# Attention with a gated feed-forward block: the low part of the probabilities times the high part of v alone, in six matmuls a head, placed by the scheduler

## The chip, the cores and the metric

The kernel runs on one core of one Trainium2 chip. The metric is the device time of one execution in microseconds (us). The kernel before took 822.91 us, the median of three runs (821.95 to 823.51). The traces come from a separate profiled execution.

Engine names are those of the profile: PE is TensorE (matmuls), PEld its weight loads, DVE VectorE, ACT ScalarE, POOL GpSimd, SP SyncE, which here issues DMAs only.

## What is computed

The reference, cut to what matters, with 8 batches, 8 heads, 576 positions and a head dimension of 64:

```python
scores = scale * np.matmul(q, k.transpose(0, 1, 3, 2))
bias = -(cum[:, :, :, None] - cum[:, :, None, :])      # cum = cumsum(max(s, 0))
scores = np.where(causal, -1000000000.0, scores + np.minimum(bias, 0.0))
attn = np.exp(scores - max); attn = attn / (sum + 1e-09)
x = np.matmul(attn, v)                                 # heads side by side: (8, 576, 512)
h = gelu(x @ w_in)                                     # 512 -> 1024
u, v = halves of h
v_n = (v - mu) / np.sqrt(var + 1e-06) * g_ln
v_s = np.einsum('ts,bsd->btd', w_sg, v_n) + b_sg[None, :, None]
return x + (u * v_s) @ w_out
```

## The kernel before, in words

**The arithmetic.** The first 12 heads (`NP`, line 50) take their probabilities and v as plain float32. For the other 52 heads both are split: a float32 number is written as a high part, rounded to the type float32r, and a low part, the rest, also float32r. The product of two such numbers is then made of matmuls of parts. The feed-forward block works in such parts throughout, with three products of four (high·high, high·low, low·high).

**One head.** `scores` (line 713) makes the score matrix in strips in the PSUM buffers `sc`; DVE adds the mask and finds the extreme, ACT makes the exponentials into the SBUF tiles `p`. `transposes` (line 744) turns 12 blocks of 128x128 of `p` round on PE (`tr`, line 749: `p` is the weight operand of 128 columns, `ident` the moving operand of 128 columns), in four PSUM tiles `pt` of 4, 4, 2 and 2 blocks. The ring `pt` has two buffers. Each tile is evacuated by `evac` (line 759): ACT writes the high part (`pah`, `pbh`, `pdh`) and DVE the low part, PSUM minus high part (`pal`, `pbl`, `pdl`). Each of these SBUF tiles exists once, so the next head overwrites it. `pv` (line 807) multiplies by v. Its PSUM tile `xx` (128 rows, 512 columns) comes from a pool of one buffer (`ps_x`, line 446); the last 64 positions go to a tile `x0` (in the profile `x`) from the ring `pt`. The weights are `vs[:, jt]`, where 64 columns of high part and 64 columns of low part of v lie side by side. One matmul with 128 weight columns thus makes high-part sums in rows 0 to 63 and low-part sums in rows 64 to 127. The high part of the probabilities and then the low part stream against these 128 columns: of low parts four matmuls, of 512, 448, 320 and 192 columns. At the end ACT copies rows 64 to 127 to SBUF (tile `xr`) and DVE adds rows 0 to 63. After every second head POOL multiplies `xr` by the reciprocal sums.

**The feed-forward block** of a batch, `ffn` (line 861), consists of units v, u, s and o, each a chain of 12 to 14 matmuls into one of three PSUM buffers (`ps_m`), in the order of the string `ORDER` (line 42). The batch of eight heads before is in the feed-forward block while the next eight heads are in attention. Matmuls are of 128 weight columns and 288 or 512 moving columns. Only the last v unit, that of 64 positions, has in each batch four matmuls with 64 weight columns and 512 moving columns (line 910).

**The order of the work.** All operations are first recorded (`Program.add`) with a key, the time in heads at which they are due (`place`, line 1009, `POS`, line 58). `Program.graph` finds the dependencies; a PSUM buffer counts as one piece there, so any two accesses of which one writes stay in the order of the recording. `Program.cost` (line 189) gives each operation a duration `d` and for PE a load time. `plan` (line 308) is a greedy list scheduler: at each step it takes, over the five engines, the ready operation with the earliest start among up to 48 a queue, the earlier key first among equals. On PE an operation starts at

```python
s = max(pest + peocc, max(at[i], pest) + cost[i][2])
```

that is, when the matmul before it has streamed (`peocc` is its `d`) and its own weights, loaded from the start of that matmul on (`cost[i][2]`), are there. `emit` (line 275) issues everything in this order. The order on each engine is then fixed on the chip; only waits move. As all instructions are issued in `emit`, the profile gives line 289 for each of them, and one goes by the names of the tiles.

Two more features of `plan` are touched. Elementwise DVE operations that read and write SBUF alone are marked `wide`; `held` and `asked` put such an operation behind a POOL operation marked `lock` that runs at the planned time, and the other way round.

Of the kernel before, what the change touches and what calls it, by code (L numbers as in the profile page):

```python
# [21 lines left out]
P = 128  # L22
# [26 lines left out]
NQ = 8  # L49
NP = 12  # L50
U2 = 8
ENG = {'k': 'sg', 'vs': 'sg', 'xs': 'gg', 'ln': 'sg', 'gt': 'sg', 'w': 'gg', 'ws': 'sv', 'ws1': 'g'}
MT = 52.0
LATE = 0.0
# [12 lines left out]
OVERLAP = [0, 93, 75, 25, 0]  # L67
MARGIN = 100.0
ISSUE = 450.0


class Buf:
# [99 lines left out]
class Program:  # L172
# [16 lines left out]
    def cost(self, op):  # L189
        e, name, ins, outs, kw = op["eng"].n, op["name"], op["ins"], op["outs"], op["kw"]  # L190
        big = [v for v in ins if v.columns() > 1]
        n = outs[0].columns() if outs else big[0].columns()
        ps = [v.buf.pool.psum for v in big]
        ops_ = bool(outs) and outs[0].buf.pool.psum
        wide = lock = False
        d, load = 50.0, 0.0
        if e == PE:
            if name == "transpose":
                d, load = 110.0, 0.44 * ins[0].columns()
            else:  # L200
                w, m = ins
                load, n = 0.84 * w.columns(), m.columns()
                d = 0.463 * n if m.dtype == F32R else max(0.833 * n, load) + 0.833 * n
        elif e == ACT:
            f = kw.get("func")
            d = (195 if not any(ps) else 166) + 0.834 * n
            if f == AF.Exp:
                d = 480 + 0.834 * n
            elif f == AF.Tanh:
                d += 10  # L210
        elif e == DVE:
            d = 150 + 1.045 * n
            if name == "tensor_tensor_reduce":
                d += 7
            elif name == "reciprocal":
                d = 170
            elif name == "bn_stats":
                d = 687
            elif name == "bn_aggr":
                d = 172  # L220
            elif name == "memset":
                d = 60 + 0.8 * n
            elif n > 1 and not ops_ and not any(ps):
                wide = True
                if len(big) == 1:
                    d = 140 + 0.53 * n
        elif e == POOL:
            lock = n > 64
            if name == "tensor_tensor":
                d = (560 if kw["op"] == ALU.pow else 193) if n == 1 else 170 + 2.17 * n  # L230
            elif name == "tensor_scalar":
                d = 255 + 0.84 * n if n > 4 else 210
                if kw["op0"] == ALU.max:
                    d, lock = 3.3 * n, False
            else:
                d, lock = 140 + n, False
        else:
            v = (outs or big)[0]
            d, load = v.dims[0][1] * v.columns() * 4 / 280.0, ISSUE
        return e, d, load, wide, lock  # L240
# [65 lines left out]


def plan(cost, pre, first, uses, order, bufs, prio, after, slack=(0, 0, 0, 0, 0), window=48):

    n = len(cost)
    left = [len(p) for p in pre]
    succ = [[] for _ in range(n)]
    for i, p in enumerate(pre):
        for q in p:
            succ[q].append(i)
    issue = [[] for _ in range(n)]
    for i, qs in after.items():  # L320
        for q in qs:
            issue[q].append(i)
            left[i] += 1
    owner, remain = {}, {}
    for i in range(n):
        for b in first[i]:
            owner[b] = i
            left[i] += 1
        for b in uses[i]:
            remain[b] = remain.get(b, 0) + 1  # L330
    ready = [[] for _ in range(5)]
    at = [0.0] * n
    tagof = {b: t for t, bs in order.items() for b in bs}
    free_slots = {t: [0.0] * bufs[t] for t in order}
    nxt = {t: 0 for t in order}
    last = {}

    def put(j):
        left[j] -= 1
        if left[j] == 0:  # L340
            insort(ready[cost[j][0]], (prio[j], j))

    def grant(t):
        while free_slots[t] and nxt[t] < len(order[t]):
            b = order[t][nxt[t]]
            nxt[t] += 1
            f = free_slots[t]
            x = min(f)
            f.remove(x)
            j = owner[b]  # L350
            at[j] = max(at[j], x)
            put(j)

    for i in range(n):
        if left[i] == 0:
            insort(ready[cost[i][0]], (prio[i], i))
    for t in order:
        grant(t)
    free = [0.0] * 5
    start, fin = [0.0] * n, [0.0] * n  # L360
    pest = peocc = moved = 0.0
    held = asked = (0.0, 0.0)
    seqs = [[] for _ in range(5)]
    for _ in range(n):
        best = None
        for e in range(5):
            cand, least = [], 1e18
            for pr, i in ready[e][:window]:
                if e == PE:
                    s = max(pest + peocc, max(at[i], pest) + cost[i][2])  # L370
                    soon = pest + peocc + 1
                else:
                    s = max(at[i], free[e])
                    soon = free[e]
                cand.append((s, pr, i))
                least = min(least, s)
                if s <= soon:
                    break
            for c in cand:
                if c[0] <= least + slack[e]:  # L380
                    if best is None or c[0] < best[0]:
                        best = (c[0], e, c[1], c[2])
                    break
        if best is None:
            return None
        s, e, pr, i = best
        del ready[e][bisect_left(ready[e], (pr, i))]
        _, d, load, wide, lock = cost[i]
        if e == PE:
            pest, peocc, end = s, d, s + d + 60  # L390
            free[e] = s
        elif e == SP:

            moved = max(moved, s + 1300) + d
            free[e], end = s + load, moved + 600
        else:
            if e == DVE and wide and held[0] <= s < held[1]:
                s = held[1]
            if e == POOL and lock and asked[0] <= s < asked[1]:
                s = asked[1]  # L400
            end = s + d
            if wide:
                asked = (s, end)
            if lock:
                held = (s, end)
            free[e] = end - OVERLAP[e]
        start[i], fin[i] = s, end
        seqs[e].append(i)
        for j in issue[i]:
            at[j] = max(at[j], s)  # L410
            put(j)
        for j in succ[i]:
            ej = cost[j][0]
            at[j] = max(at[j], s if e == ej == PE else end + LATENCY[e][ej] + MARGIN)
            put(j)
        for b in uses[i]:
            remain[b] -= 1
            last[b] = max(last.get(b, 0.0), end)
            if remain[b] == 0:
                free_slots[tagof[b]].append(last[b] + 60)  # L420
                grant(tagof[b])
    return max(fin), start, fin, seqs
# [3 lines left out]
def tile_attn_gmlp(  # L426
# [380 lines left out]
    def pv(h):  # L807
# [5 lines left out]
        if key not in xr:  # L813
            xr[key] = moe.tile([P, S], F32, name="xr", tag="xr", bufs=8)
        xt = xr[key]
        parts = 1 if f32 else 2
        rows = D if f32 else P

        def st(jt):
            return d["v"][:, jt, :] if f32 else d["vs"][:, jt, :, :].rearrange("p a d -> p (a d)")  # L820

        xx = ps_x.tile([P, 512], F32, name="xx", tag="xx")

        def mm(o0, o1, jt, m, **kw):
            nc.tensor.matmul(xx[0:rows, o0:o1], st(jt), m, **{"start": False, "stop": False, **kw})

        m, pb, pd = pt["pa"], pt["pb"], pt["pd"]
        for k in range(parts):  # L830
            mm(0, 512, 0, m[k], start=(k == 0))
        yield 0.2
        for k in range(parts):
            mm(64, 512, 1, pb[k][:, 320:768])
        for k in range(parts):
            mm(128, 448, 2, pb[k][:, 0:320])
        yield 0.65
        mm(192, 384, 3, pd[0][:, 128:320])
        if not f32:
            mm(192, 384, 3, pd[1])  # L840
        x0 = ps_pt.tile([P, 512], F32, name="x0", tag="pt")
        if f32:
            nc.tensor.matmul(xx[0:rows, 256:320], st(4)[REM:P], pd[0][REM:P, 64:128], start=False, stop=True)
            nc.tensor.matmul(x0[0:rows, 0:64], st(5)[0:REM], pd[0][0:REM, 64:128], start=True, stop=True)
        else:
            mm(256, 320, 4, pd[0][:, 0:64], stop=True)
            nc.tensor.matmul(x0[:, 0:64], st(5), pd[0][:, 64:128], start=True, stop=True)
        hs = slice(64 * half, 64 * half + 64)
        for ps, o, sl in ((x0, slice(0, 64), slice(512, S)), (xx, slice(0, 512), slice(0, 512))):
            if f32:  # L850
# [257 lines left out]
```

## Time and profile before

| what | value |
|---|---|
| median of three runs | 822.91 us |
| the profiled execution | 821.75 us |
| its span, first to last instruction | 820.0 us |
| outside the span | 1.75 us |
| matmuls, and as many weight loads | 5129 |
| granted TensorE clock, mean | 0.997 |
| transposes, 128x128 | 768, mean 276 ns |
| low-part matmuls of 52 heads | 208 |

A matmul's duration in the profile runs from its issue to a modelled end, and matmuls overlap. What a matmul takes of the engine is read from the distance between starts in a timeline, not from its duration. A matmul that follows a transpose is recorded some 28 ns after the start of that transpose and then lasts longer. In rows such as `128*64 128x512` the first pair is weight rows and columns, the second the moving operand.

### The profile page before, as it was taken

How to read it: one execution, taken by the hardware profiler on the slowest of the kernel's cores; microseconds unless marked ns; L12 is line 12 of the kernel's file. 1: busy time of each engine (PE TensorE's matmuls, PEld its weight loads, DVE VectorE, ACT ScalarE, POOL GpSimd, SP SyncE). 2: the span in 40 equal slices, each digit the busy share in tenths (PEclk: the TensorE clock that was granted, in tenths of full speed). 3: DMA queues.
4: the chain of work that ended last, by engine and by line, in shares of the span. 5: the costliest groups of instructions: out<-in, count | busy, mean ns of one | idle time of the engine just before them, and what ended most of it. 6: DMA issues, size and time to landing. Idle time of an engine off the chain costs nothing.

```text
span 820.0 us, 16771 instructions
## 1 busy us (share of the span) xinstructions
PE 791.2 (96%) x5129; PEld 687.4 (84%) x5129; DVE 614.2 (75%) x1845; ACT 574.1 (70%) x1576; POOL 497.2 (61%) x767
## 2 busy tenths in 40 slices
PE   7999989999999999999999999999999999999998
PEld 4455557999988998899988998889988998889998
DVE  5798489877797678875788677976788767884662
ACT  4777679867787577876687677875778866872350
POOL 3676679584467555585476745675555854746442
PEclk9999999999999999999999999999999999999999
DMA  7576754555425654354535554256443546321101
GB/s 226 160 222 164 173 158 112 128 136 141 115 65 132 165 129 117 88 137 111 148 93 130 137 128 119 68 128 170 122 120 89 138 113 152 85 51 44 43 8 59
DMA packets 75566, 98.91 MB, mean 121 GB/s; under 512 B 27298, under 2 KB 43876, under 8 KB 75476
## 3 DMA queue, kind: packets, MB, share of 16 engines
q1 hardware_dynamic: 75476, 97.84, 45.7%
q8 instruction: 41, 0.67, 0.4%
q14 instruction: 49, 0.40, 0.2%
HBM read 51.71 MB, written 9.90 MB: 75 GB/s over the span
## 4 chain that ended last, share of the span: by engine, by line
PE 83%; DVE 7%; ACT 3%; DMA 3%; issue 3%; POOL 1%; SPq 0%; ACTq 0%; POOLq 0%; DVEq 0%
PE sm L289 13%; PE om L289 13%; PE sc L289 12%; PE vm L289 12%; PE xx L289 11%; PE um L289 10%; PE pt L289 10%; DVE p L289 2%; ACT p L289 1%; DMA raw<-in_kq 1%; PE x L289 1%; DVE u L289 1%; DVE bs L289 1%; DVE vm L289 1%; DVE vt L289 1%
## 5 line engine op out<-in xcount | busy, mean ns | idle before, releaser
L289 ACT ACTIVATE p<-p,mn 128x320 f32<-128x320 f32 (+4 forms) x320 | 177.8, 557 | 42.3 <-DVE mn L289 38.9
L289 PE MATMUL pt<-ident,p 128*128 128x128 f32 x768 | 156.6, 276 | 4.7 <-ACT pal L289 1.4
L289 DVE CUSTOM_DVE_ANT_0 p<-sc,mask 128x448 f32<-128x448 f32 (+4 forms) x320 | 125.2, 421 | 25.4 <-PE sc L289 22.9
L289 PE MATMUL sc<-k,q 66*128 66x288 f32 (+9 forms) x672 | 134.5, 307 | 2.2 <-DMA k<-cum 1.3
L289 PE MATMUL sm<-ws,vn 128*128 128x288 f32 x768 | 134.2, 304 | 2.3 <-DVE u L289 2.3
L289 PE MATMUL um<-xs,wi 128*128 128x288 f32 x768 | 132.0, 306 | 1.4 <-DVE u L289 1.1
L289 PE MATMUL om<-gt,wo 128*128 128x288 f32 x768 | 131.0, 307 | 0.0
L289 PE MATMUL vm<-wi,xs 128*128 128x512 f32 (+1 forms) x416 | 126.8, 408 | 0.1
L289 PEld LDWEIGHTS pt<-ident,p 128*128 128x128 f32 x768 | 97.6, 140 | 28.5 <-issue 5.6
L289 PEld LDWEIGHTS sm<-ws,vn 128*128 128x128 f32 x768 | 112.2, 188 | 6.3 <-DVE u L289 4.9
L289 PEld LDWEIGHTS um<-xs,wi 128*128 128x128 f32 x768 | 110.7, 189 | 4.2 <-DVE vt L289 2.1
L289 PEld LDWEIGHTS sc<-k,q 128*128 128x128 f32 (+3 forms) x672 | 101.4, 181 | 13.1 <-DVE mn L289 3.7
L289 PEld LDWEIGHTS om<-gt,wo 128*128 128x128 f32 x768 | 109.3, 189 | 1.1
L289 POOL TENSOR_TENSOR k<-raw,k 128x576 fp32r<-128x576 f32 x56 | 80.3, 1434 | 32.0 <-ACT k L289 19.7
L289 POOL TENSOR_TENSOR gt<-u,gt 128x288 fp32r<-128x288 f32 x64 | 50.8, 808 | 57.9 <-ACT gt L289 55.8
L289 PEld LDWEIGHTS vm<-wi,xs 128*128 128x128 f32 (+1 forms) x416 | 71.2, 185 | 10.8 <-DVE vt L289 0.4
L289 DVE SCALAR_TENSOR_TENSOR u<-u,um 128x288 f32<-128x288 f32 x128 | 56.5, 441 | 10.5 <-ACT u L289 10.2
L289 POOL TENSOR_SCALAR bs<-bs 128x1 f32<-128x1 f32 (+1 forms) x80 | 17.2, 215 | 77.3 <-DVE bs L289 74.1
L289 ACT CAST pbh<-pt 128x512 fp32r<-128x512 f32 x104 | 49.4, 481 | 19.5 <-PE pt L289 18.5
L289 POOL TENSOR_SCALAR p<-p 64x64 f32<-64x64 f32 x128 | 32.2, 252 | 49.4 <-ACT p L289 36.7
L289 POOL TENSOR_TENSOR xr<-xr,rb 128x576 f32<-128x576 f32 x32 | 46.1, 1441 | 24.0 <-DMA rb<-rd 20.6
L289 ACT ACTIVATION_READ_ACCUMULATOR p<-p,mn 128x1 f32 (+1 forms) x320 | 60.2, 188 | 0.0
(123 smaller groups left out, 1645.5 us busy)
## 6 DMA issues: line engine op xcount, KB each, us to landing
q<-k SPq DMA_DIRECT2D x168, 144.0 KB
raw<-in_kq SPq DMA_DIRECT2D x56, 288.0 KB
vr<-in_vp SPq DMA_DIRECT2D x52, 192.0 KB
rb<-rd SPq DMA_DIRECT2D x64, 144.0 KB
out_t<-ot SPq DMA_DIRECT2D x64, 144.0 KB
k<-k SPq DMA_DIRECT2D x56, 144.0 KB
wraw<-in_w_in SPq DMA_DIRECT2D x16, 256.0 KB
kf<-in_kq SPq DMA_DIRECT2D x8, 288.0 KB
```

Of the source, the lines that this page charges most:

```text
L289: r = getattr(op["eng"].real, op["name"])(*[f(a) for a in op["args"]], **{k: f(v) for k, v in op["kw"].items()})
```

## The change: six low-part matmuls of 64 weight columns

In `pv`, for the 52 split heads, the low part of the probabilities is multiplied by the high part of v alone: weights `vs[:, jt, 0, :]`, 64 columns, output rows 0 to 63. The four low-part matmuls become six, of 256, 256, 224, 224, 320 and 192 columns, the same 1472 columns in all. They are recorded after all other matmuls of the head but one: first the high parts, then the `x0` matmul, then the six, and last the matmul of 64 columns that closes `xx`.

In `cost` a transpose gets `d` 59 and a load of 0.84 ns a column (107.5 ns) in place of 110 and 56. Matmuls in float32r with 64 weight columns and more than 64 moving columns are marked: the six, and the four of the last v unit. In `plan` a marked matmul is put 60 ns (`WAIT`) later in the comparison of starts as long as transposes remain and the matmul before it is not a transpose. DVE operations between SBUF tiles get other durations, plain float32 matmuls slightly longer ones, and the use of `held` and `asked` is removed.

```diff
+LOW = ((0, 0, "a", 0, 256), (256, 0, "a", 256, 512), (64, 1, "b", 320, 544), (288, 1, "b", 544, 768),
+       (128, 2, "b", 0, 320), (192, 3, "d", 0, 192))
...
+WAIT = 60.0
...
             if name == "transpose":
-                d, load = 110.0, 0.44 * ins[0].columns()
+                d, load = 59.0, 0.84 * ins[0].columns()
             else:
                 w, m = ins
                 load, n = 0.84 * w.columns(), m.columns()
-                d = 0.463 * n if m.dtype == F32R else max(0.833 * n, load) + 0.833 * n
+                wide = w.columns() == 64 and n > 64 and m.dtype == F32R
+                d = 0.463 * n if m.dtype == F32R else max(0.84 * n, load) + 0.84 * n + 70
...
                 wide = True
-                if len(big) == 1:
-                    d = 140 + 0.53 * n
+                d = 155 + 1.62 * n if len(big) > 1 else 250 + 0.8 * n
...
+    after_t = was_t = False
+    turns = sum(c[2] > 60 > c[1] > 50 for c in cost if c[0] == PE)
...
+                if e == PE and cost[i][3] and not after_t and turns:
+                    s += WAIT
                 cand.append((s, pr, i))
...
         if e == PE:
-            pest, peocc, end = s, d, s + d + 60
+            after_t = load > 60 > d > 50
+            if wide and not was_t and turns:
+                s -= WAIT
+            turns -= after_t
+            was_t = after_t
+            pest, peocc, end = s, d, s + max(d, 110.0) + 60
             free[e] = s
...
-            if e == DVE and wide and held[0] <= s < held[1]:
-                s = held[1]
-            if e == POOL and lock and asked[0] <= s < asked[1]:
-                s = asked[1]
             end = s + d
...
-        m, pb, pd = pt["pa"], pt["pb"], pt["pd"]
-        for k in range(parts):
-            mm(0, 512, 0, m[k], start=(k == 0))
+        pa, pb, pd = pt["pa"], pt["pb"], pt["pd"]
+        mm(0, 512, 0, pa[0], start=True)
         yield 0.2
-        for k in range(parts):
-            mm(64, 512, 1, pb[k][:, 320:768])
-        for k in range(parts):
-            mm(128, 448, 2, pb[k][:, 0:320])
+        mm(64, 512, 1, pb[0][:, 320:768])
+        mm(128, 448, 2, pb[0][:, 0:320])
         yield 0.65
         mm(192, 384, 3, pd[0][:, 128:320])
-        if not f32:
-            mm(192, 384, 3, pd[1])
...
         else:
+            nc.tensor.matmul(x0[:, 0:64], st(5), pd[0][:, 64:128], start=True, stop=True)
+            for lo, jt, m, m0, m1 in LOW:
+                mm(lo, lo + m1 - m0, jt, {"a": pa, "b": pb, "d": pd}[m][1][:, m0:m1], 1)
             mm(256, 320, 4, pd[0][:, 0:64], stop=True)
-            nc.tensor.matmul(x0[:, 0:64], st(5), pd[0][:, 64:128], start=True, stop=True)
```

In the new `mm` the last argument `k=1` selects the 64 columns of high part of v and rows 0 to 63 of `xx`.

More of the change, by code (lines that the diff above doesn't have):

```diff
@@ L815, in pv, with st, mm @@
         xt = xr[key]
[L816 to L820, printed above, removed]
+        def st(jt, k=0):
+            if f32:
+                return d["v"][:, jt, :]
+            return d["vs"][:, jt, 0, :] if k else d["vs"][:, jt, :, :].rearrange("p a d -> p (a d)")
         xx = ps_x.tile([P, 512], F32, name="xx", tag="xx")
-        def mm(o0, o1, jt, m, **kw):
-            nc.tensor.matmul(xx[0:rows, o0:o1], st(jt), m, **{"start": False, "stop": False, **kw})
-        m, pb, pd = pt["pa"], pt["pb"], pt["pd"]
-        for k in range(parts):
-            mm(0, 512, 0, m[k], start=(k == 0))
+        def mm(o0, o1, jt, m, k=0, **kw):
+            rows = D if f32 or k else P
+            nc.tensor.matmul(xx[0:rows, o0:o1], st(jt, k), m, **{"start": False, "stop": False, **kw})
+        pa, pb, pd = pt["pa"], pt["pb"], pt["pd"]
+        mm(0, 512, 0, pa[0], start=True)
         yield 0.2
-        for k in range(parts):
-            mm(64, 512, 1, pb[k][:, 320:768])
-        for k in range(parts):
-            mm(128, 448, 2, pb[k][:, 0:320])
+        mm(64, 512, 1, pb[0][:, 320:768])
+        mm(128, 448, 2, pb[0][:, 0:320])
         yield 0.65
         mm(192, 384, 3, pd[0][:, 128:320])
-        if not f32:
-            mm(192, 384, 3, pd[1])
         x0 = ps_pt.tile([P, 512], F32, name="x0", tag="pt")
         if f32:
-            nc.tensor.matmul(xx[0:rows, 256:320], st(4)[REM:P], pd[0][REM:P, 64:128], start=False, stop=True)
-            nc.tensor.matmul(x0[0:rows, 0:64], st(5)[0:REM], pd[0][0:REM, 64:128], start=True, stop=True)
-        else:
+            nc.tensor.matmul(xx[0:D, 256:320], st(4)[REM:P], pd[0][REM:P, 64:128], start=False, stop=True)
+            nc.tensor.matmul(x0[0:D, 0:64], st(5)[0:REM], pd[0][0:REM, 64:128], start=True, stop=True)
+        else:
+            nc.tensor.matmul(x0[:, 0:64], st(5), pd[0][:, 64:128], start=True, stop=True)
+            for lo, jt, m, m0, m1 in LOW:
+                mm(lo, lo + m1 - m0, jt, {"a": pa, "b": pb, "d": pd}[m][1][:, m0:m1], 1)
             mm(256, 320, 4, pd[0][:, 0:64], stop=True)
-            nc.tensor.matmul(x0[:, 0:64], st(5), pd[0][:, 64:128], start=True, stop=True)
         hs = slice(64 * half, 64 * half + 64)
```

## The prediction

> **What bounds the kernel now.** First the page's head, then busy time by stretches of 82 us.
>
> ```profile
> span 820.0 us, 16771 instructions
> PE 791.2 (96%) x5129; PEld 687.4 (84%) x5129; DVE 614.2 (75%) x1845; ACT 574.1 (70%) x1576; POOL 497.2 (61%) x767
> PE 83%; DVE 7%; ACT 3%; DMA 3%; issue 3%; POOL 1%; SPq 0%; ACTq 0%; POOLq 0%; DVEq 0%
> ```
>
> ```profile
> 0.00:82.00 82.00, 73.36 (x320) 41.79 (x320) 62.09 (x188) 54.29 (x163) 50.70 (x75) 1.00 0.69 193
> 82.00:164.00 82.00, 74.79 (x444) 56.77 (x443) 65.38 (x203) 63.98 (x182) 59.27 (x93) 0.98 0.57 143
> ...
> 328.00:410.00 82.00, 80.56 (x557) 73.95 (x555) 62.24 (x193) 60.79 (x169) 49.29 (x71) 1.00 0.47 121
> ```
>
> The first number after the length of a stretch is PE's busy time. PE is the bound: it is busy 96% of the span and is 83% of the chain that ended last. It has gaps of 8.6 and 7.2 us in the first two stretches and of 1.4 us in a later one, and in all of 820.0 - 791.2 = 28.8 us. This is the least that PE idles, since busy time counts overlapping records. So the change is worth what it takes from the time that PE streams, and what its new order does to PE's gaps. No other engine is full.
>
> **What PE pays for each kind of work.** Three stretches of PE's timeline show it, in which starts are compared.
>
> ```profile
> 769.87 2.96 PE L289 MATMUL vm<-wi,xs 128*128 128x512 f32 x12
> 772.67 3.36 PE L289 MATMUL um<-xs,wi 128*128 128x288 f32 x24
> 775.87 2.50 PE L289 MATMUL vm<-wi,xs 128*128 128x512 f32 x10
> ```
>
> ```profile
> 402.27 0.49 PE L289 MATMUL pt<-ident,p 128*128 128x128 f32 x3
> 402.52 0.48 PE L289 MATMUL vm<-wi,xs 128*128 128x512 f32 x1
> 402.84 0.27 PE L289 MATMUL pt<-ident,p 128*128 128x128 f32 x1
> ```
>
> ```profile
> 119.37 0.49 PE L289 MATMUL pt<-ident,p 128*128 128x128 f32 x3
> 119.62 0.48 PE L289 MATMUL vm<-wi,xs 128*64 128x512 f32 x1
> 119.94 0.27 PE L289 MATMUL pt<-ident,p 128*128 128x128 f32 x1
> 119.96 0.47 PE L289 MATMUL vm<-wi,xs 128*64 128x512 f32 x1
> 120.27 0.39 PE L289 MATMUL vm<-wi,xq 128*128 128x512 f32 x1
> ```
>
> Twelve matmuls of 512 columns take 772.67 - 769.87 = 2.80 us, 0.233 us each, or 0.455 ns a column. Three transposes in a row last 0.49 us where the last alone lasts 0.27, so they follow each other at 0.11 us.
>
> The question of the change is what the 0.11 us are. If a transpose streams for about 0.06 us (128 columns at 0.455 ns) and the rest is the wait for the next 128 weight columns, a matmul of 64 columns behind it starts 0.05 us sooner. If it streams for 0.11 us itself, the weights behind it do not matter. The second and third fence decide it. At 402.27 the last of three transposes starts at 402.27 + 0.49 - 0.27 = 402.49, a matmul of 128 weight columns and 512 moving ones follows, and the next transpose starts at 402.84: 0.35 us for the pair. At 119.37 the last of three starts at 119.59, a matmul of the same 512 moving columns but 64 weight columns follows, and the next transpose starts at 119.94: again 0.35 us. The pair behind that one takes 120.27 - 119.94 = 0.33. With 0.233 for the stream, the transpose takes 0.10 to 0.12 in each. A short transpose would have made the two pairs with 64 columns 0.06 + 0.23 = 0.29.
>
> Two more readings agree, the time of weight loads and of plain float32 matmuls of the first heads.
>
> ```profile
> L289 PEld LDWEIGHTS pt<-ident,p 128*128 128x128 f32 x768 | 97.6, 140 | 28.5 <-issue 5.6 <-ACT pal L289 2.0 <-POOL bs L289 2.0
> ...
> L289 PEld LDWEIGHTS sm<-ws,vn 128*128 128x128 f32 x768 | 112.2, 188 | 6.3 <-DVE u L289 4.9
> ...
> L289 PEld LDWEIGHTS vm<-wi,xs 128*64 128x64 f32 x32 | 4.3, 135 | 1.2
> ```
>
> ```profile
> 32.69 0.92 PE L289 MATMUL sc<-kf,qf 128*128 128x448 f32 x2
> 33.45 0.27 PE L289 MATMUL pt<-ident,p 128*128 128x128 f32 x1
> ```
>
> A transpose's weights load in 140 ns, like 64 columns of other weights (135) and 48 ns sooner than 128 (188). Transposes in a row therefore do not wait for their loads. And plain float32 operands, which a transpose has, stream at (33.45 - 32.69) / (2 x 448) = 0.85 ns a column, and 128 of these are 0.109 us. The Trainium skill, "TensorE: Matmul & The Clock Gate", section "LDWEIGHTS (loading the stationary operand)", says that a load takes its columns divided by 1.2 in ns, 107 ns for 128 and 53 for 64, and its section "Back-to-back issue gap" gives 134 cycles, 56 ns, for 128 moving columns alone. By these two together a transpose would be short, the 0.11 us would be the load behind it, and the change would gain. The rows with 64 columns above disagree: 0.35 and 0.33 us against 0.29.
>
> **The change part by part.** *The low-part matmuls.* They lose 64 weight columns and keep their moving columns: 512 + 448 + 320 + 192 = 1472 before, 256 + 256 + 224 + 224 + 320 + 192 = 1472 after, 0.67 us a head both times. Two more matmuls a head cost the fixed part of a matmul. The 24 of 288 columns above, (775.87 - 772.67) / 24 = 0.133 us each, and the 0.233 for 512 give 0.446 ns a column and 5 ns fixed. A matmul must also hide the load behind it, about 108 ns for 128 columns by the rows (twice 188 - 135). Pieces of 224 columns stream 105 ns, 3 ns short, twice a head. Together 52 x (2 x 5 + 2 x 3) ns = +0.8 us. Evacuations, the work of the softmax and the DMAs stay as many and as large as they were: the low-low product shared its PSUM tile with the others, so its end frees no other engine.
>
> *The pieces behind transposes.* By the rows above this gains nothing: 0 us. The lowest it could cost is the design's own 0.05 us a piece, -0.05 x 6 x 52 = -15.6 us, which I treat as a rival.
>
> *The order in time.* The pieces now stand behind all high parts of the head, so they wait for the next head's transposes while other work is ready. One head and the start of the next:
>
> ```profile
> 410.13 0.27 PE L289 MATMUL x<-pdh,vs 128*128 128x64 f32 x1
> 410.43 0.28 PE L289 MATMUL pt<-ident,rs 128*10 128x128 f32 x1
> 410.46 0.34 PE L289 MATMUL xx<-pdl,vs 128*128 128x192 f32 x1
> ...
> 414.55 0.49 PE L289 MATMUL pt<-ident,p 128*128 128x128 f32 x3
> ...
> 416.71 0.27 PE L289 MATMUL pt<-ident,p 128*128 128x128 f32 x1
> ...
> 417.86 0.27 PE L289 MATMUL pt<-ident,p 128*128 128x128 f32 x1
> ...
> 418.21 0.38 PE L289 MATMUL pt<-ident,p 128*128 128x128 f32 x2
> ...
> 419.58 0.39 PE L289 MATMUL xx<-pah,vs 128*128 128x512 f32 x1
> ```
>
> Before, the last low part is issued at 410.46. After, three pieces can go behind the transposes at 414.55 and the others behind those from 416.71 on, so `xx` closes near 418 in place of 410.7. Feed-forward matmuls move forward into the place left, and 0.67 us of work changes place without a cost of its own, as long as such matmuls are ready. If that cover is gone, the 0.67 us stand open, which the rival below prices.
>
> *The planner's belief.* It will count a piece behind a transpose 0.05 us too short, up to 0.3 us a head, 15.6 us in all. On the chip PE will then lag behind its plan, and DVE and ACT results arrive earlier against it. Gaps such as that at 410.13, where 64 columns (0.03 us) are followed 0.30 us later by the next matmul, 0.27 us idle, can close. The lowest value is nothing gained; the highest is 52 x 0.27 = 14 us. Not all gaps stand behind a piece, and a list scheduler given shorter work also packs tighter, so I take a quarter of 15.6, -3.9 us.
>
> *DVE's durations and the two locks.* They concern SBUF-only operations, mostly those that prepare weights in the first 164 us.
>
> ```profile
> L289 DVE SCALAR_TENSOR_TENSOR wbits<-wraw,wbits 128x256 int32<-128x256 int32 x48 | 27.3, 573 | 0.4
> ```
>
> ```profile
> L289 DVE SCALAR_TENSOR_TENSOR wbits<-wraw,wbits x48: 407/423/1778, 15.2 to 150.2; 128x256 int32<-128x256 int32 x48
> ```
>
> The old formula gives 150 + 1.045 x 256 = 418 ns, the median; the new one 155 + 1.62 x 256 = 570, the mean. The mean is right for a sum, the median with the lock for each single instruction. So the new order can gain or lose there. Its bounds are the gaps of the first two stretches, a tenth of 15.8 us either way; I take 0. The 32 matmuls of the last v units are marked too: at most 32 x 0.06 = 1.9 us if nothing else were ready, taken at 0 since PE goes to other work.
>
> The sum against the profiled execution is 821.75 + 0.8 - 3.9 = 818.6 us. That execution lies 1.16 us below the median of the three runs, so against the median it is **819.8 us**.
>
> **The rivals.** *The order gains nothing.* Without the 3.9 us the sum is 822.9 + 0.8 = 823.7 us, no change that can be told. For it: the new list has its own gaps.
>
> *One buffer too few: slower.* `xx` has one buffer, and the next head's first matmul into it waits until ACT and DVE have emptied it.
>
> ```profile
> L289 ACT COPY xr<-xx x64: 577/582/586, 23.1 to 743.5; 64x512 f32<-64x512 f32 x64
> ...
> L289 DVE TENSOR_TENSOR xr<-xx,xr x52: 648/682/685, 136.4 to 744.1; 64x512 f32<-64x512 f32 x52
> ```
>
> These are 0.58 + 0.68 us and a few tenths in the queues of ACT and DVE, which at that time evacuate transposes. The high part of the next head is due at 419.58, so the point from which it decides is a close of `xx` later than about 418.1. A sixth piece behind the transposes at 418.21 passes it by 0.3 us or more, and the whole chain of high parts slips. Where feed-forward matmuls cover it, it costs nothing; uncovered in a quarter of the heads at the 0.3 us plus one evacuation of 0.58, it is 13 x 0.88 = 11 us, of which I count 4, because PE also gives back some of it in later gaps: 823.7 + 4 = 827.7, up to 835 in full. Against it: PE has feed-forward work ready in nearly all of that stretch.
>
> *The load is hidden after all.* 823.7 - 15.6 = 808 us. Against it stand the two pairs with 64 columns; for it, only that they are two.
>
> **How the numbers follow.** A measurement of this kernel tells 0.2%, 1.6 us, from no change: below 821.3 or above 824.5. The forecast (815 to 821.3) has a chance of 0.37, the order that gains nothing 0.20, the missing buffer 0.35, the hidden load 0.08. Faster is 0.37 + 0.08 = 0.45, the same 0.20, slower 0.35. The range 811 to 831 leaves out the hidden load, the top of the missing buffer (0.07) and a little of the forecast's lower end. The forecast's own range is 815 to 821.3.
>
> **What would show it.** In the changed profile a transpose with a piece of 256 columns behind it should take 0.11 + 0.119 = 0.23 us to the next start; 0.18 would be the hidden load. The six groups should show 64 weight columns and loads of 135 ns, `xx` should close behind the next head's transposes, and the gap behind the matmul into `x` should shrink from 0.27 us. If `xx<-pah` waits for DVE's or ACT's emptying of `xx`, and PE's busy time in the stretch from 328 us on falls below 80 us in 82, the missing buffer has come true. The prediction is wrong in its main step if PE streams less per head than before.

## The result: slower by 0.6%, and the profile after

| | before | changed |
|---|---|---|
| median of 11 runs each | 822.91 us | 828.07 us |
| lowest and highest | 821.78 and 825.23 | 825.05 and 831.48 |
| ratio of the changed to before | | 1.0062 (95%: 1.0042 to 1.0081) |
| profiled execution, its span | 821.75, 820.0 us | 826.84, 825.1 us |

The change lost 5 us where 3 were to be gained. The two profiled executions differ by 5.1 us, and the traces show where most of these went. First the head of the page of the changed kernel and its busy time by stretches (PE's busy time is the first number after the length; the last three numbers are granted clock, DMA share and GB/s).

```profile
span 825.1 us, 16907 instructions
PE 795.2 (96%) x5233; PEld 693.7 (84%) x5233; DVE 618.3 (75%) x1845; ACT 576.9 (70%) x1576; POOL 493.9 (60%) x767
```

```profile
82.00:164.00 82.00, 76.16 (x442) 58.26 (x443) 64.84 (x199) 62.50 (x177) 56.83 (x90) 0.96 0.53 139
...
410.00:492.00 82.00, 79.61 (x555) 72.76 (x554) 63.94 (x199) 61.60 (x168) 51.66 (x81) 1.00 0.50 128
492.00:574.00 82.00, 79.62 (x551) 72.60 (x550) 64.01 (x198) 61.33 (x167) 51.17 (x79) 1.00 0.46 116
```

There are 104 matmuls more, two for each of the 52 heads, and PE idles 825.1 - 795.2 = 29.9 us by its records, 1.1 more than before. PE's gap is now 2.0 to 2.4 us in the four stretches of 82 from 410 us on, where 1.4 was quoted before. The records alone would thus put 4.0 of the 5.1 us down to longer busy time. They overlap, and their ends are modelled, so what is work and what is gap is taken from starts below.

**The granted clock has a part in the loss.** The eleven runs of the changed kernel had a mean granted clock, as a share of the full one, from 0.990 to 0.998, with a median of 0.994. If the lost share costs its full share of the span, an estimate, that is 0.006 x 826.4 = 5.0 us in the median run. The runs bear the estimate out: the one at 0.998 took 825.12 us, the one at 0.990 took 831.48, 6.4 us more where 0.008 x 826 is 6.6. Of the kernel before, only the profiled execution's clock is on record with this result, 0.997; in its 102 runs beside the experiments the median is 1.000. The profiled executions had 0.997 and 0.996, so some 0.8 of their 5.1 us is clock and the rest must be something else.

**Where the time went.** The last transpose of a kernel starts at 741.0 us before and at 746.6 after; what follows, the rest of the feed-forward blocks, takes 79.0 and 78.5 us. Up to there both kernels nearly repeat themselves from batch to batch. The rows are the first transposes of heads 24 (the 289th of all), 32 and 40. Before:

```profile
267.04 0.28 PE L289 MATMUL pt<-ident,p 128*128 128x128 f32 x1
...
362.47 0.27 PE L289 MATMUL pt<-ident,p 128*128 128x128 f32 x1
...
458.00 0.27 PE L289 MATMUL pt<-ident,p 128*128 128x128 f32 x1
```

After:

```profile
268.23 0.30 PE L292 MATMUL pt<-ident,p 128*128 128x128 f32 x1
...
363.89 0.30 PE L292 MATMUL pt<-ident,p 128*128 128x128 f32 x1
...
460.63 0.30 PE L292 MATMUL pt<-ident,p 128*128 128x128 f32 x1
```

From head 32 to head 40, 95.53 us became 96.74. To split such a batch into work and gaps, every matmul in it was given what the prediction worked out: 109 ns for a transpose, 5 ns and 0.446 ns a column for the others, and no less than the load behind it (107 ns for 128 weight columns, 54 for 64). What a start comes later than that is a gap. This gives 90.0 us of work and 5.5 of gaps before, 90.2 and 6.5 after. The work grew by 0.2 us a batch, near the 8 x 16 ns foretold. The gaps grew by 1.0. The clock is 1.00 in both.

Not every batch lost so much. From head 24 to head 32 it is 95.43 us before and 95.66 after, the added work and nothing else. The three batches from head 32 to head 56 lost 1.2, 1.3 and 1.0 us, 3.5 us together; another 1.2 us was lost before head 24.

**The pieces behind transposes** are where they were meant to be. One head of the changed kernel:

```profile
403.04 0.27 PE L292 MATMUL pt<-ident,p 128*128 128x128 f32 x1
403.07 0.36 PE L292 MATMUL xx<-pal,vs 128*64 128x256 f32 x1
403.27 0.27 PE L292 MATMUL pt<-ident,p 128*128 128x128 f32 x1
403.30 0.36 PE L292 MATMUL xx<-pal,vs 128*64 128x256 f32 x1
403.50 0.27 PE L292 MATMUL pt<-ident,p 128*128 128x128 f32 x1
```

Each transpose with a piece of 256 columns takes 0.23 us to the next start, as the prediction said for a transpose that streams 0.11 us itself; the hidden load would have made it 0.18.

**A wait that was not there before.** PE's waits from 330 to 738 us, before and after (total, times, longest):

```profile
PE xx L289 <- ACT pah L289: 3.0, 5, 0.6
PE sm L289 <- DVE u L289: 1.9, 5, 0.4
PE pt L289 <- DVE bs L289: 0.9, 5, 0.2
```

```profile
PE sc L292 <- DMA k<-k: 3.4, 3, 1.3
PE xx L292 <- ACT pbh L292: 1.4, 5, 0.3
PE xx L292 <- ACT pah L292: 1.0, 1, 1.0
...
```

In three batches, at 446, 543 and 639 us, the score matmuls now wait for the copy of k. The issues of SP around the first of them, and the matmul, before and then after:

```profile
436.51 0.31 SPq L289 DMA_DIRECT2D rd<-rt  x1
...
439.31 0.47 SPq L289 DMA_DIRECT2D k<-k  x1
439.82 1.31 SPq L289 DMA_DIRECT2D rb<-rd  x2
...
444.77 0.37 PE L289 MATMUL sc<-k,q 128*128 128x448 f32 x1
```

```profile
431.56 0.33 SPq L292 DMA_DIRECT2D vr<-in_vp  x1
436.18 0.30 SPq L292 DMA_DIRECT2D rd<-rt  x1
...
438.98 1.25 SPq L292 DMA_DIRECT2D rb<-rd  x2
440.32 0.53 SPq L292 DMA_DIRECT2D vr<-in_vp  x1
440.95 0.48 SPq L292 DMA_DIRECT2D k<-k  x1
...
446.09 0.47 PE L292 MATMUL sc<-k,q 128*128 128x448 f32 x1 [1.23 <-DMA k<-k]
```

After, SP issues nothing from 431.9 to 436.18: the next in its order is `rd<-rt`, the reciprocal sums, which come by way of DVE, and SP's own waits from 434 to 447 us name DVE:

```profile
SPq L292 <- DVE xr L292: 4.5, 1, 4.5
```

Then the two `rb<-rd` stand ahead of `k<-k`, not behind it. `k<-k` goes out 1.6 us later than before, but the batch began 1.4 us later too: measured from the first transpose of head 32, it goes out at 76.84 us before and at 77.06 after. What moved is the order on PE. Before, the score matmul came 5.46 us after the issue; after, PE is ready for it after 3.91 us and has to wait until 5.14. By the starts this place costs 4.2 us in the three batches, which is more than the 3.5 us by which they are longer. One batch earlier the distances are the same and the wait is not there:

```profile
345.31 0.48 SPq L292 DMA_DIRECT2D k<-k  x1
...
349.34 0.47 PE L292 MATMUL sc<-k,q 128*128 128x448 f32 x1
```

Here the copy was there at most 4.03 us after its issue, and this is the batch that lost only 0.2 us. So the new order left the copy too little room, and where it took longer PE waited. Why it took longer in the three batches is not known. This is read from the trace and was not tried by itself, and it is a place and not yet a cause: the order of all queues changed at once.

### The profile page after: what moved, and what is told of

It reads as the page before. It is cut to its first block, busy times and chain, and to the rows that moved or that the text cites. A ratio compares the mean times of both kernels' runs of the same rounds, so it can differ in the third digit from the quotient of the medians.

```text
span 825.1 us, 16907 instructions
## 1 busy us (share of the span) xinstructions
PE 795.2 (96%) x5233; PEld 693.7 (84%) x5233; DVE 618.3 (75%) x1845; ACT 576.9 (70%) x1576; POOL 493.9 (60%) x767
## 4 chain that ended last, share of the span: by engine, by line
PE 74%; DVE 8%; ACT 8%; DMA 4%; issue 2%; POOL 2%; SPq 1%; DVEq 0%; POOLq 0%; ACTq 0%
PE sm L292 12%; PE om L292 12%; PE sc L292 11%; PE vm L292 10%; PE xx L292 9%; PE pt L292 9%; PE um L292 8%; DMA k<-k 3%; DVE wbits L292 2%; DVE p L292 2%; SPq L292 1%; ACT pdh L292 1%; ACT p L292 1%; ACT vt L292 1%; ACT u L292 1%
## 5 line engine op out<-in xcount | busy, mean ns | idle before, releaser
L292 PE MATMUL pt<-ident,p 128*128 128x128 f32 x768 | 170.9, 279 | 6.5 <-DVE pal L292 1.8
L292 PE MATMUL sc<-k,q 66*128 66x288 f32 (+9 forms) x672 | 140.1, 309 | 5.7 <-DMA k<-k 4.3
L292 PE MATMUL sm<-ws,vn 128*128 128x288 f32 x768 | 130.7, 301 | 0.4 <-DVE u L292 0.4
L292 PEld LDWEIGHTS pt<-ident,p 128*128 128x128 f32 x768 | 100.1, 141 | 31.5 <-issue 12.2
L292 PE MATMUL vm<-wi,xs 128*128 128x512 f32 (+1 forms) x416 | 124.9, 408 | 0.2 <-POOL xs L292 0.2
L292 PEld LDWEIGHTS sc<-k,q 66*128 66x128 f32 (+3 forms) x672 | 103.6, 182 | 19.0 <-DMA k<-k 4.5
L292 PEld LDWEIGHTS um<-xs,wi 128*128 128x128 f32 x768 | 112.4, 192 | 3.9 <-DVE u L292 2.3
L292 PEld LDWEIGHTS sm<-ws,vn 128*128 128x128 f32 x768 | 110.2, 189 | 1.1 <-DVE u L292 0.5
L292 POOL TENSOR_TENSOR vs<-vr,vs 128x384 fp32r<-128x384 f32 x52 | 52.7, 1013 | 39.4 <-ACT vs L292 39.3
L292 DVE TENSOR_TENSOR pbl<-pt,pbh 128x512 fp32r<-128x512 f32 x104 | 56.7, 550 | 8.8 <-ACT pbh L292 6.0
```

What stands on the lines that cost most here:

```text
L292: r = getattr(op["eng"].real, op["name"])(*[f(a) for a in op["args"]], **{k: f(v) for k, v in op["kw"].items()})
```

## The experiments

Theory when they began: PE's work is the same, and the new order makes gaps. Rivals: the weight loads do matter; the late pieces and the single `xx` buffer make the gaps; the wrong duration of a transpose (59 ns) in the scheduler makes them; the DVE durations and the missing locks make them. All times are medians, the ratio is to the kernel before on the same chip, with its 95% interval. The kernels ran on several chips, so two of them are best compared by their ratios.

### The width of the weights

**e1, the pieces with 128 columns in the same order.** Of the product it computes the low-low part too.

```diff
-            rows = D if f32 or k else P
+            rows = D if f32 else P
-            return d["vs"][:, jt, 0, :] if k else d["vs"][:, jt, :, :].rearrange("p a d -> p (a d)")
+            return d["vs"][:, jt, :, :].rearrange("p a d -> p (a d)")
```

`cost` still counts 64 columns for them, so that the order stays the same.

> The changed kernel with the six low-part pieces at the same places in the same order on every engine, but with 128 weight columns (high and low part of v) in place of 64, so that only the weight load behind each transpose doubles. If a transpose streams for 0.11 us itself and hides the load, the time is that of the changed kernel within 1.5 us (826 to 830), and a transpose with a piece of 256 columns behind it takes the same 0.23 us. If the load behind a transpose were what is paid, each piece would cost 0.05 us more, 15 us in all: about 842.

830.5 us, 1.0094 (1.0076 to 1.0113). This is 11.5 us short of the 842 of the load's price and 0.5 us above the band of the other. The same place of its timeline:

```profile
405.08 0.27 PE L292 MATMUL pt<-ident,p 128*128 128x128 f32 x1
405.11 0.37 PE L292 MATMUL xx<-pal,vs 128*128 128x256 f32 x1
405.32 0.27 PE L292 MATMUL pt<-ident,p 128*128 128x128 f32 x1
405.34 0.37 PE L292 MATMUL xx<-pal,vs 128*128 128x256 f32 x1
405.55 0.27 PE L292 MATMUL pt<-ident,p 128*128 128x128 f32 x1
```

0.235 us a pair with twice the weight columns, against 0.23. The load behind a transpose is hidden at both widths. In this trace the clock is 0.93 from 600 to 650 us, which is 3.5 us of clock, where that of the changed kernel is 1.00. So the excess over the band need not be the load's.

**e12, 64 columns in the old places.** The four low-part matmuls stay between the high parts, under the scheduler of before.

```diff
-            mm(0, 512, 0, m[k], start=(k == 0))
+            mm(0, 512, 0, m[k], k, start=(k == 0))
```

(and so for the other three)

> The scheduler of before with the four low-part matmuls where they stood, between the high parts, but with 64 weight columns and 64 output rows. If fewer weight columns gain nothing, 821 to 824. If they gain by themselves, 818 to 820.

821.22 us, 0.9982 (0.9968 to 0.9996): no gain that can be told from the scatter below.

### The product by v and the scheduler apart

**e2** takes `pv` of before and the changed scheduler; **e3** takes the changed `pv` and the scheduler of before (in which no piece prefers a transpose); **e8** is e3 with 128 weight columns, low-low part computed.

> The changed scheduler (durations, the 60 ns, no locks) with the product by v of before: four low-part matmuls of 128 columns among the high parts. If the late pieces and the single xx buffer make the loss, this is back at 822 to 824. If the scheduler's new durations make it, it stays at 826 to 829.

827.77 us, 1.0066 (1.0044 to 1.0088): the loss with the product by v of before.

> The scheduler of before with the new product by v: six pieces of 64 columns recorded behind the other matmuls of the head, no preference for transposes. If the late pieces make the loss, 826 to 829. If the scheduler's durations make it, 822 to 824.

818.32 us, 0.9952 (0.9933 to 0.9970): faster than both kernels.

> The scheduler of before, with the six pieces recorded late as in the new product by v, but with 128 weight columns. If the gain of 4 us comes from the pieces being free to fill gaps at the end of the head, 817 to 820. If it comes from the 64 columns, whose load is 54 ns shorter, 821 to 823.

821.57 us, 0.9986 (0.9974 to 0.9998). This lies in the band that was given to the 64 columns, but e10 below, with 64 columns, took 823.62 us, so it does not show them to be the cause.

The loss is in the scheduler's part. e3 does not try the late pieces, though they are recorded last in it: without the 60 ns the planner puts them among the high parts, and `xx` closes long before the next head needs it.

```profile
410.41 0.22 PE L291 MATMUL xx<-pdh,vs 128*128 128x64 f32 x1
...
419.94 0.40 PE L291 MATMUL xx<-pah,vs 128*128 128x512 f32 x1
```

From 330 to 738 us the median distance between these two is 7.0 us in e3, 7.1 before, 7.2 in e2 and 2.4 in the changed kernel. So against the missing buffer speaks e2, which loses as much with 7.2 us. A batch of e3, from the first transpose of head 32 to that of head 40:

```profile
364.10 0.27 PE L291 MATMUL pt<-ident,p 128*128 128x128 f32 x1
...
458.04 0.38 PE L291 MATMUL pt<-ident,p 128*128 128x128 f32 x2
```

93.94 us, of which 89.9 are work and 4.1 gaps by the same count.

### The scheduler's parts one by one

e5, e6 and e7 add one part each to e3. e5 also has the 70 ns that the change adds to plain float32 matmuls, and e5 and e7 have the planned end of a matmul that the change brings (`max(d, 110.0)` in place of `d`). These two were not tried alone.

```diff
 e5: +                if e == PE and cost[i][3] and not after_t and turns:
     +                    s += WAIT
     +                d = 0.463 * n if m.dtype == F32R else max(0.84 * n, load) + 0.84 * n + 70
     +            pest, peocc, end = s, d, s + max(d, 110.0) + 60
 e6: +                d = 155 + 1.62 * n if len(big) > 1 else 250 + 0.8 * n
     -            if e == DVE and wide and held[0] <= s < held[1]: ...
 e7: -                d, load = 110.0, 0.44 * ins[0].columns()
     +                d, load = 59.0, 0.84 * ins[0].columns()
     +            pest, peocc, end = s, d, s + max(d, 110.0) + 60
```

> The scheduler of before and the new product by v (818.3 in the run of that alone), and added to it only the 60 ns by which marked matmuls are put back unless a transpose stands before them; transposes count 110 ns. If holding the pieces back for transposes is what loses in the steady batches (94.0 us a batch without it), about 821 and a batch near 96. If it is harmless, 817 to 819.5.

824.67 us, 1.0031 (1.0018 to 1.0044), a batch (head 32 to head 40) of 96.3 us.

> The scheduler of before and the new product by v, and added to it only the new durations of DVE operations between SBUF tiles and the missing locks. These act in the first 165 us, where weights are prepared. If the locks are what the first part needs, 820 to 824 with the loss before 175 us and batches of 94.0 after it. If they are harmless, 817 to 819.5.

827.02 us, 1.0055 (1.0037 to 1.0072). The loss was expected in the first 165 us. The batch takes 96.1 us in place of 93.94, so at least part of it stands later. The median clock of its runs is 0.993.

> The scheduler of before and the new product by v, and added to it only the belief that a transpose takes 59 ns and its load 107.5. If this belief is the main loss (the changed kernel came down from 828 to 821 without it), 822 to 826. If it loses only together with the 60 ns, 817 to 820.

840.49 us, 1.0221 (1.0206 to 1.0235), a batch of 97.7 us. The median clock of its runs is 0.985, and 0.015 x 839 = 12.6 us of its loss are clock by the estimate above. In it and in e6 `xx` closes 7.7 us (median) before the next head needs it, so these lose without late pieces too.

Each part alone loses, and the three together lose less than the third alone. They do not add up.

### The duration of a transpose in the scheduler

**e4** is the changed kernel with 110 ns and a load of 56 in `cost`, pieces still preferred behind transposes.

> The changed kernel, still with pieces preferred behind transposes, but the scheduler again counts a transpose as 110 ns with a load of 56 ns. If the belief of 59 ns makes PE lag behind its plan and that costs, this is at 822 to 825. If the belief is harmless, it stays at 826 to 829. If the lag helps, as my forecast had it, it is slower than the changed kernel, 830 or more.

820.83 us, 0.9985 (0.9972 to 0.9999). Its pieces are as late as those of the changed kernel (2.3 us from the close of `xx` to the next head's first matmul), so late pieces need not lose. With e7 the duration looked like the cause. Four more kernels vary the two numbers of that line: 109 and 56 (e13), 59 and 56 (e14), 110 and 107.5 (e15), 135 and 56 (e16). In e4, e5 and these four the test for a transpose goes by the duration, so that the 32 small transposes of the sums count as transposes as well.

> The changed kernel, pieces still preferred behind transposes, with a transpose counted as 109 ns and its load as 56 (e4 had 110 and 56 and took 820.8). If the true duration is what brought the time down, 819 to 825 again. If e4 was a lucky order, 826 to 831.

826.98 us, 1.0058 (1.0035 to 1.0081).

> The changed kernel with the duration of 59 ns kept and the load put back to 56. A row of transposes then counts 0.06 us each where PE takes 0.11, so the plan runs ahead of PE at every transpose and not only before pieces. If a plan that runs ahead of PE is what costs, this is worse than the changed kernel: 832 to 842. If the long load costs, 820 to 824.

827.05 us, 1.0047 (1.0032 to 1.0062).

> The changed kernel with the true duration of 110 ns and the long load of 107.5 kept. If the short duration costs, 819 to 825. If the long load costs, 826 to 831.

829.84 us, 1.0082 (1.0064 to 1.0099).

> The changed kernel with a transpose counted as 135 ns, 26 too long, and a load of 56. If only a plan that runs ahead of PE costs, 819 to 825. If any wrong duration costs, 826 or more.

825.83 us, 1.0031 (1.0018 to 1.0043).

The theory of the wrong duration falls as the whole cause. With 109 ns, what PE takes, the kernel is where it was; e4 was a lucky order. Its batch takes 96.2 us, that of e13 96.4, so e4 did not win by its batches; its median clock is 1.000, that of e13 0.997.

### One nanosecond

These change the scheduler's transpose by 1 ns and nothing else: before (e9), e3 (e10) and the changed kernel (e11).

> The kernel before with one number changed: the scheduler counts a transpose as 109 ns in place of 110, a change that means nothing on the chip but gives another order. If the scheduler's order is stable, 822 to 823. If any small change moves it by several us, the time lies anywhere from 817 to 828, and effects of that size in the other runs say nothing of their causes.

822.89 us, 1.0005 (0.9992 to 1.0018).

> The scheduler of before and the new product by v (818.3), with 109 in place of 110 for a transpose. If the gain of the new product by v is real, 816 to 820. If it was a lucky order, up to 826.

823.62 us, 1.0021 (1.0006 to 1.0035).

> The changed kernel with 58 in place of 59 for a transpose. If the loss of the changed kernel has a cause in the wrong duration, 826 to 830. If it was an unlucky order, down to 820.

830.54 us, 1.0093 (1.0078 to 1.0108).

A nanosecond that means nothing moves e3 by 5.3 us and e4 (to e13) by 6.2; it moves the changed kernel by 2.5 and the kernel before by nothing that can be told. The gain of e3 is therefore an order too. A batch of e10:

```profile
363.67 0.38 PE L291 MATMUL pt<-ident,p 128*128 128x128 f32 x2
...
459.60 0.27 PE L291 MATMUL pt<-ident,p 128*128 128x128 f32 x1
```

95.93 us against 93.94, with the same 89.9 us of work: 2 us of gaps a batch from one nanosecond in the plan.

### The DVE durations and the locks

**e17** is the changed kernel with these two put back as before, **e18** the same with 58 ns for a transpose.

> The changed kernel with the old durations of DVE operations between SBUF tiles and the two locks put back, everything else changed. If the DVE part makes the loss, 820 to 825. If the loss is in the other parts or in the chance of an order, 826 to 831.

826.66 us, 1.0053 (1.0029 to 1.0076). One of its eleven executions took 1494.38 us and is not in the ratio.

> The same with 58 in place of 59 ns for a transpose, to give a second order. If the DVE part makes the loss, 820 to 825 again. If chance rules, it may differ from the run before it by up to 5 us.

825.17 us, 1.0043 (1.0027 to 1.0060). Not the cause by themselves either.

## Why the prediction was wrong, point by point

**What PE pays for a transpose: right, and shown.** 0.11 us of its own, whatever weights are loaded behind it: 0.23 us with a piece of 256 columns, with 64 and with 128 weight columns (e1). The hidden load, given 0.08, did not come. The Trainium skill's 107 ns for 128 columns and 53 for 64 ("TensorE: Matmul & The Clock Gate", section "LDWEIGHTS (loading the stationary operand)") agree with the slope of the recorded loads, 188 - 135 = 53 ns for 64 columns. But this time is not on PE's path behind a transpose, so the gain that one would work out from it is not there.

**The work on PE: right.** +0.8 us was forecast for 52 heads, 16 ns a head; the batches show 0.2 us for eight. One number of that sum was off: twice 188 - 135 is 106 ns for a load, not 108, which takes 0.2 us from the 0.8.

**The planner's belief: this step failed.** "On the chip PE will then lag behind its plan", the prediction says, so that gaps close: -3.9 us. This term alone made the forecast a gain. The gap at `x` that it named did close: from the start at 410.13 to the next it was 0.30 us, and at the same place after, 411.31, it is 0.03. But others opened, at 424.97 behind `x` again with 0.39 us, and the gaps of a batch grew in all. No run shows the belief to gain: it costs 22 us in e7 against e3, and 17 against e10, and in the changed kernel correcting it gives 7 us in e4 and 1 us in e13. In place of the gain the runs show a scatter that the prediction did not have. Any edit of the scheduler's numbers gives another order, and orders with nearly the same work lie from 818 to 840 us. The prediction treated the order as a small correction with a known sign, and the bounds of the term (0 to -14) left out a loss. Its sum has no term for the granted clock either.

**The order that gains nothing: the nearest in mechanism.** It gave 823.7 and had 0.20, and said that the new list has its own gaps. It has, but the sum put them at nothing, and the changed kernel lies 4.4 us above it.

**The missing buffer: near the time, not the mechanism.** It gave 827.7 and had 0.35. `xx` does close behind the next head's transposes. Its last matmul of head 35 and the first of head 36, in the changed kernel:

```profile
418.83 0.21 PE L292 MATMUL xx<-pdh,vs 128*128 128x64 f32 x1
...
421.06 0.40 PE L292 MATMUL xx<-pah,vs 128*128 128x512 f32 x1
```

The limit named was 418.1, but the changed kernel's batch began 1.4 us later. Measured from the first transpose of head 32, `xx` closes at 54.94 us where the limit was 55.63, and the first matmul of the next head comes at 57.17 where it came at 57.11. So this head did not slip. No gap is recorded before it, none of PE's waits above is for the emptying of `xx`, e4 with pieces as late is not slower, and e2, e6 and e7 lose without late pieces. One sign that was named did come, less than 80 us of busy time in 82; it tells of gaps and not of their cause. The wait that can be named is for the copy of k, which the prediction did not look at.

**DVE's durations and locks: taken at 0.** With them alone e6 lost 8.7 us against e3 and 3.4 against e10. Put back alone, they return nothing that can be told: 1.0053 in e17 and 1.0062 in the changed kernel, with intervals that overlap.

**What is shown and what stays open.** All kernels fall in two groups. The scheduler of before, with either product by v: 1, 1.0005, 0.9952, 1.0021, 0.9986, 0.9982. Any of the three scheduler edits: 14 kernels, one at 0.9985 and 13 from 1.0031 to 1.0221. So the loss is in the scheduler's edits. It is not work: it comes as gaps in the order and as clock. How it divides differs from kernel to kernel. By the median clocks of the runs, the estimate above gives 0 us of clock in e5 (1.000), 1.7 in e14 (0.998), 5.8 in e6 (0.993) and 6.6 in e15 (0.992). Which edit it is stays open: each loses alone, none wins the time back reliably when it is undone, and 1 ns moves single orders by as much as 6 us. That the other constants of the kernel fit the old scheduler is a thought that no run here tests.

## What to carry to other kernels

Measure what an instruction takes between starts, with both neighbours that matter, before a rule on loads is built on it: two pairs of rows in the trace before were enough to see that this idea hides nothing. When a greedy scheduler fixes the order of five engines, a change of its costs or of what it places is a draw from a scatter (here -0.5% to +2.2%) around the work; perturb a number that means nothing, by 1 ns, and read single results against that spread before giving them a cause. Put the granted clock beside every time, and look whether an experiment built what its name says (e3 has no late pieces) before it is used against a rival. A faster version found in one order (e3) is worth keeping as an order, but it is no proof of the edit that made it.

## What the hardware showed that was not expected

Some short gaps of PE cost clock. In the changed kernel, stretches of 5 us around two gaps:

```profile
125.00:130.00 5.00, 4.58 (x34) 4.05 (x32) 3.94 (x15) 4.39 (x13) 4.83 (x12) 1.00 0.65 186
130.00:135.00 5.00, 3.24 (x16) 2.76 (x17) 4.93 (x11) 2.84 (x9) 5.00 (x9) 0.79 0.26 56
135.00:140.00 5.00, 5.00 (x37) 5.00 (x35) 4.39 (x17) 4.57 (x14) 2.81 (x4) 0.87 0.47 118
140.00:145.00 5.00, 3.44 (x19) 2.87 (x18) 4.89 (x11) 4.38 (x11) 2.11 (x6) 0.82 0.02 5
145.00:150.00 5.00, 5.00 (x33) 4.69 (x32) 3.08 (x11) 2.93 (x9) 2.65 (x5) 0.84 0.38 98
```

PE is idle for 1.76 us in the second of them, and the mean granted clock falls to 0.79 there and 0.87 in the next, although PE is busy again; 5 x (0.21 + 0.13) = 1.7 us of clock are lost. The trace has 3.4 us at half: the clock is 0.50 from 132.92 to 136.33 us and again, behind the gap near 142 us, from 143.16 to 146.57. A gap of 1 to 2 us can thus cost twice, and part of the scatter between runs of one order is clock. But not every such gap costs: behind the waits of 1.23 and 1.25 us at 446 and 543 us the clock stays at 1.00. In e15 the same gap of 1.54 us comes six times, once a batch; in the 5 us behind it the clock is 0.66 at 341 and at 535 us, and 1.00 at 244, 439, 632 and 729. What decides between them is not shown here.
